# Zero fills of a gradient kernel: fifteen instead of thirteen with 8 KB rows, and whole heads in one transfer

## Chip, cores, metric

One core of one Trainium2 chip. The metric is the device time of the whole kernel in microseconds (us). It is the median of several executions.

## The reference, cut

The kernel computes one decode step of a block (attention with a sliding window, then a gated FFN) and all of its gradients. What matters here is the size of two of the outputs:

```python
Hq, Hkv, Sk, Dh = 16, 8, 32768, 256
W = min(4096, max(256, Sk // 4))                     # 4096
k = jnp.repeat(k_cache[:, :, Sk - W:, :], rep, axis=1)
v = jnp.repeat(v_cache[:, :, Sk - W:, :], rep, axis=1)
...
_out, _vjp = jax.vjp(_f, A_x, A_k_cache, A_v_cache, A_wq, A_wo, B_w_gate, B_w_up, B_w_down)
```

Only the last 4096 of 32768 positions of each cache are read, so seven eighths of both cache gradients are zero. They are outputs nevertheless: 2 x 8 x 28672 x 256 bf16 values, 234.9 MB of zeros out of 280.6 MB that the kernel writes.

## The kernel before

The zeros come from an on-chip tile of 128 partitions x 16 KB. A "block" of zeros is 128 rows of 16 KB, 2.097 MB; a head of one output has seven blocks. GpSimd's queue (`ZQ`) carries most of the fills. SyncE's queue (`LD`) carries loads, results and a few late fills.

```python
ZW = 8192
HALF0, HALF1 = 42, 55
GROUP = 4
...
def send_fills(n0, n1, halves=False):
    while n0 < n1:
        o, g, i = fills[n0]
        n = 1
        while n < GROUP and n0 + n < n1 and fills[n0 + n][:2] == (o, g):
            n += 1
        reg = zero_rows(o, g, i, i + n, ZW)
        if halves:                       # each 16 KB row as twice the lower 8 KB of the tile
            for r in range(n):
                ZQ.dma_start(out=reg[r].rearrange("p (k f) -> p k f", k=2), in_=zeros[:, 0:ZW // 2].unsqueeze(1).to_broadcast([128, 2, ZW // 2]))
        elif n == 1:
            ZQ.dma_start(out=reg[0], in_=zeros)
        else:
            ZQ.dma_start(out=reg.rearrange("n p f -> p n f"), in_=zeros.unsqueeze(1).to_broadcast([128, n, ZW]))
        n0 += n

send_fills(0, HALF0)                     # 42 blocks, 16 KB rows
send_fills(HALF0, HALF1, True)           # 13 blocks, 8 KB rows: "half fills"
# ... attention; in the FFN stage the upper half of the zero tile holds a block of weights ...
            if n == 1:
                nc.vector.memset(ar(ZW // 2, ZW // 2), 0.0)      # L443: upper half is zero again
                send_fills(HALF1, len(fills) - 1)                # the rest, 16 KB rows
# ... at the end: the last block in four pieces (L673, GpSimd), late fills (L680, SyncE)
```

A fill is only issued while fewer than eight transfers of its queue are open; the ninth waits for the first to land. In the trace of the kernel before, eight go out from 5.1 us on and the ninth at 40.5 us, after a wait for a landing.

Of the kernel before, what the change touches and what calls it, by code (L numbers as in the profile page):

```python
# [24 lines left out]
EPS = 1e-5  # L25
SCALE = 1.0 / 16.0
ZW = 8192
HALF0, HALF1 = 42, 55
GROUP = 4
NZ = (Sk - W) * Dh // (128 * ZW)  # L30
KB = 512

# [2 lines left out]
def kernel(  # L35
# [93 lines left out]
# [6 lines that stand above are left out]
# [575 lines left out]
```

## Time and profile before

| | before |
|---|---|
| time | 796.63 us median of 4 (795.74 to 797.07) |
| span of the traced execution | 796.7 us (this execution took 798.43 us) |
| moved by DMA | 334.75 MB, 420 GB/s on average |
| busy: PE, DVE, ACT | 59%, 52%, 25% |
| GpSimd's queue (q0), SyncE's queue (q1) | 216.01 MB, 116.68 MB |

The page's part 2 cuts the span into 40 slices and gives, for each, how full the DMA engines were and what they moved; its lines, and those of the hole in the middle, are shown with the prediction. How to read them: with the DMA engines at their 430 GB/s nearly everywhere, the time is bytes over rate, and only places where the rate is lower can be won back. One such place lies near 380 us.

### The profile page before, as it was taken

To read this page: it belongs to the slowest core of one execution; us is meant where nothing else is said; L and a number is where in the kernel's file an instruction comes from. 1 tells how busy PE (TensorE), PEld (TensorE's weight loads), DVE (VectorE), ACT (ScalarE), POOL (GpSimd) and SP (SyncE) were. 2 spreads that over 40 slices of the span, in tenths; PEclk is the share of its full clock that TensorE was granted. 3 is DMA by queue.
4 is the path that set the end of the run, shared out by engine and by line. 5 is a ranking of instruction groups with operands and counts; after the bars stand their busy time and mean duration, and the time that the engine had idled before them with its cause. 6 is when DMAs were issued, how large, how long until landed. Compare 5 with 4: busy or idle time off the path is not lost.

```text
span 796.7 us, 7253 instructions
## 1 busy us (share of the span) xinstructions
PE 470.7 (59%) x2926; PEld 218.9 (27%) x2926; DVE 410.4 (52%) x621; ACT 196.0 (25%) x309; POOL 35.4 (4%) x52
## 2 busy tenths in 40 slices
PE   0359998999999999353227658583450553361000
PEld 0233433344343433141116524241110211130000
DVE  2106673846648475152883488377661584472200
ACT  0043223142240301000101217372330343162200
POOL 5000000000000000100300000000000000010000
PEclk9988999999999999755557969796565556685555
DMA  9999999999999999999899999999999999999997
GB/s 349 429 431 429 429 431 430 429 430 431 429 429 430 424 425 423 416 421 422 349 421 406 429 428 428 430 431 428 426 425 432 424 429 427 427 422 410 428 443 327
DMA packets 28680, 334.75 MB, mean 420 GB/s; under 512 B 2143, under 2 KB 5223, under 8 KB 7143
## 3 DMA queue, kind: packets, MB, share of 16 engines
q0 software_dynamic: 15824, 216.01, 64.0%
q1 hardware_dynamic: 11382, 116.68, 34.9%
q10 hardware_dynamic: 1440, 1.61, 0.6%
q8 instruction: 23, 0.38, 0.2%
q14 instruction: 11, 0.08, 0.0%
HBM read 53.69 MB, written 280.59 MB: 420 GB/s over the span
## 4 chain that ended last, share of the span: by engine, by line
another core or an unknown queue 36%; DMA 29%; DVE 14%; PE 9%; issue 2%; POOL 1%; ACT 1%; DVEq 0%; ACTq 0%; SPq 0%; POOLq 0%
DMA out_dram<-arena 29%; DVE arena L469 2%; DVE arena L658 2%; DVE arena L554 2%; PE rows_ps L266 2%; PE dqb_ps L512 2%; DVE arena L659 2%; PE d_ps L651 2%; PE tr_ps L263 1%; DVE arena L524 1%; DVE arena L438 1%; POOL out_dram L138 1%; PE dqb_ps L515 1%; DVE arena L623 1%
## 5 line engine op out<-in xcount | busy, mean ns | idle before, releaser
L322 DVE TENSOR_TENSOR arena<-arena,p_f 128x2048 bf16<-128x2048 bf16 x64 | 145.3, 2286 | 64.9 <-PE M_ps L327 64.8
L327 PE MATMUL M_ps<-arena 128*128 128x512 bf16 x512 | 129.6, 382 | 0.2 <-ACT arena L333 0.2
L651 PE MATMUL d_ps<-arena 32*128 32x512 bf16 x256 | 44.8, 507 | 104.8 <-DVE arena L659 90.3
L263 PE MATMUL tr_ps<-ident_bf,arena 128*128 128x128 bf16 x1024 | 90.6, 238 | 20.0 <-DMA arena<-in_A_k_cache_dram 12.3
L266 PE MATMUL rows_ps<-arena,vpad 128*16 128x512 bf16 x256 | 87.3, 436 | 22.1 <-DVE arena L623 16.1
L263 PEld LDWEIGHTS <-arena 128*128 128x128 bf16 x1024 | 67.0, 106 | 72.8 <-issue 59.2
L280 ACT COPY arena<-tr_ps 128x1024 bf16<-128x1024 bf16 x64 | 61.8, 1016 | 69.9 <-PE tr_ps L263 69.9
L330 PE MATMUL ok_ps<-arena 128*16 128x512 bf16 x256 | 63.8, 381 | 0.9 <-DVE arena L307 0.9
L655 ACT CAST arena<-d_ps 128x512 bf16<-128x512 f32 x64 | 37.7, 588 | 103.4 <-PE d_ps L651 103.4
L327 PEld LDWEIGHTS <-arena 128*128 128x128 bf16 x512 | 43.4, 99 | 59.2 <-issue 23.5
L621 ACT COPY arena<-tr_ps 128x1024 bf16<-128x1024 bf16 x32 | 32.5, 1016 | 108.1 <-PE tr_ps L263 48.3
L659 DVE CAST arena<-d_ps 128x512 bf16<-128x512 f32 x64 | 43.5, 679 | 20.8 <-DMA out_dram<-arena 20.8
L658 DVE CAST arena<-d_ps 128x512 bf16<-128x512 f32 x64 | 43.8, 684 | 16.1 <-PE d_ps L651 15.6
L651 PEld LDWEIGHTS <-arena 32*128 32x128 bf16 x256 | 10.6, 95 | 129.9 <-issue 80.0
L656 ACT CAST arena<-d_ps 128x512 bf16<-128x512 f32 x64 | 38.2, 596 | 22.0 <-DMA out_dram<-arena 22.0
L266 PEld LDWEIGHTS <-vpad 128*16 128x16 bf16 x256 | 18.7, 91 | 57.7 <-issue 49.5
L330 PEld LDWEIGHTS <-arena 128*16 128x16 bf16 x256 | 19.1, 89 | 41.5 <-issue 20.4
L142 POOL DMA_DIRECT2D out_dram<-arena x25 | 19.3, 775 | 230.3 <-DMA out_dram<-arena 230.2
L549 DVE TENSOR_SCALAR arena<-arena,xT 128x1792 bf16<-128x1792 bf16 (+1 forms) x9 | 7.7, 881 | 35.5 <-DMA out_dram<-arena 35.5
L295 ACT ACTIVATE e_f<-cols_ps,nbias 128x32 f32<-128x32 f32 x16 | 4.5, 285 | 86.8 <-DVE nbias L291 86.8
L524 DVE CUSTOM_DVE_ANT_0 arena<-arena 128x4096 bf16<-128x4096 bf16 x3 | 13.1, 4423 | 23.2 <-ACT arena L517 23.2
L268 DVE COPY arena<-rows_ps 16x512 f32<-16x512 f32 x16 | 10.8, 676 | 27.5 <-PE rows_ps L266 27.5
(199 smaller groups left out, 388.6 us busy)
## 6 DMA issues: line engine op xcount, KB each, us to landing
out_dram<-arena POOLq DMA_DIRECT2D x13, 8192.0 KB, 167.9
out_dram<-arena POOLq DMA_DIRECT2D x12, 6144.0 KB, 171.5
out_dram<-arena SPq DMA_DIRECT2D x18, 2048.0 KB, 26.7
out_dram<-arena POOLq DMA_DIRECT2D x14, 2048.0 KB, 59.6
arena<-in_A_v_cache_dram SPq DMA_DIRECT2D x10, 2048.0 KB, 52.7
arena<-in_A_k_cache_dram SPq DMA_DIRECT2D x8, 2048.0 KB, 31.9
out_dram<-arena SPq DMA_DIRECT2D x4, 4096.0 KB, 29.9
arena<-in_A_wq_dram SPq DMA_DIRECT2D x2, 3072.0 KB, 21.3
```

Of the source, the lines that this page charges most:

```text
L263: nc.tensor.transpose(tr_ps[:, dh, i, :], X_sb[:, 4 * q + i, dh * 128:(dh + 1) * 128], ident_bf[:])
L266: nc.tensor.matmul(rows_ps[:], lhsT=pad[:, dh, 16 * q:16 * q + 16], rhs=XT[:, dh].rearrange("p t k -> p (t k)"), start=(q == 0 and dh == 0 ...
L280: sT_ps = dots(kv_at(K_off[g]), KT_slot, vpad[g % 2], rows1, ps_c, "cols", lambda q, XT, ps: nc.scalar.copy(out=XT, in_=ps))
L322: nc.vector.tensor_tensor(out=pK, in0=K_sb[:, 4 * c:4 * c + 4, :].unsqueeze(2).to_broadcast([128, 4, 2, Dh]), in1=p_f[:, c::8, :].unsqueez ...
L327: nc.tensor.matmul(M_ps[:, vh, :], lhsT=V_sb[:, t, vh * 128:(vh + 1) * 128], rhs=pK[:, i, :, :].rearrange("p h d -> p (h d)"), start=(t == ...
L330: nc.tensor.matmul(ok_ps[:].rearrange("p k d -> p (k d)"), lhsT=ppad[g % 2][:, 8 * (t % 4) + t // 4, :], rhs=both(g, t), start=(g == 0 and ...
L621: nc.scalar.copy(out=XT, in_=ps)
L651: nc.tensor.matmul(d_ps[:, qi].rearrange("p w d -> p (w d)"), lhsT=rTm[32 * q:32 * (q + 1), l, :], rhs=R_sb[32 * q:32 * (q + 1), :], start ...
L655: nc.scalar.copy(out=stV[:, t:t + 2, :], in_=d_ps[:, :, 0, :])
L656: nc.scalar.copy(out=stK[:, t:t + 2, :], in_=d_ps[:, :, 1, :])
L658: nc.vector.tensor_copy(out=stV[:, t:t + 2, :], in_=d_ps[:, :, 0, :])
L659: nc.vector.tensor_copy(out=stK[:, t:t + 2, :], in_=d_ps[:, :, 1, :])
```

## The change

The intent: keep GpSimd's queue fed with half fills until the upper half of the zero tile is free again, and send a head's seven blocks as one transfer of 14.7 MB instead of 8.4 + 6.3 MB.

```diff
-HALF0, HALF1 = 42, 55
-GROUP = 4
+HALF0, HALF1 = 42, 57
+GROUP = 7
```

## The prediction

> **What bounds the kernel now.** I read the page's part 2 first, because it says for every fortieth of the span whether anything is full.
>
> ```profile
> DMA  9999999999999999999899999999999999999997
> GB/s 349 429 431 429 429 431 430 429 430 431 429 429 430 424 425 423 416 421 422 349 421 406 429 428 428 430 431 428 426 425 432 424 429 427 427 422 410 428 443 327
> HBM read 53.69 MB, written 280.59 MB: 420 GB/s over the span
> ```
>
> The DMA engines are full in every slice but three, while part 1 has PE at 59% and DVE at 52%. So the span is a number of bytes over a rate: 334.75 MB at the 429 GB/s of a good slice is 780.3 us, and the other 16 us are where the rate was lost. Three slices (19.9 us each) stand out. The first, at 349, is the start: 19.9 x (1 - 349/429) = 3.7 us. The last, at 327, is the drain: 4.7 us. The twentieth, at 349, is a hole in the middle of the kernel: again 3.7 us. The remaining 4 us are spread over the stages with slightly lower rates.
>
> Next the hole, in the busy times by stretches (columns: stretch, its length, PE, PEld, DVE, ACT, POOL busy, granted clock, DMA share, GB/s).
>
> ```profile
> 370.00:375.00 5.00, 2.60 (x29) 2.28 (x30) 0.00 (x0) 0.00 (x0) 0.00 (x0) 0.50 1.02 428
> 375.00:380.00 5.00, 1.06 (x13) 0.91 (x12) 3.53 (x6) 0.00 (x0) 0.00 (x0) 0.50 1.00 424
> 380.00:385.00 5.00, 0.82 (x3) 0.33 (x4) 4.55 (x12) 0.00 (x0) 1.15 (x2) 0.50 0.35 144
> 385.00:390.00 5.00, 3.35 (x22) 2.20 (x21) 3.65 (x11) 1.01 (x1) 4.71 (x7) 0.50 0.99 378
> ```
>
> From about 380.5 to 385 the DMA engines have next to nothing. The timeline of GpSimd and DVE says why (start, length, engine, line, operation, count, idle before and its releaser).
>
> ```profile
> 340.11 0.67 POOL L138 DMA_DIRECT2D out_dram<-arena  x1 [5.53 <-DMA out_dram<-arena]
> 381.79 1.76 DVE L443 MEMSET arena<- 128x2048 uint32 x1 [0.41 <-DVE hh_f L424]
> 383.85 0.55 POOL L140 DMA_DIRECT2D out_dram<-arena  x1 [43.07 <-DVE arena L443]
> 384.39 5.32 POOL L142 DMA_DIRECT2D out_dram<-arena  x7
> ```
>
> The upper half of the zero tile is lent to weights. While it is, GpSimd may only send "half" fills, which read the lower half twice in 8 KB rows (L138, thirteen of them). The last was issued at 340.1; the next fill needs the memset at L443, done at 383.5, and goes out at 383.85. The DMA view for 376 to 380 has 99.7% of the engines' time on queue 0, GpSimd's: no other queue has work here, so when the thirteenth half fill is through, the engines stop. The rest of the FFN stage is not a reason to be idle; there is simply nothing queued.
>
> Last, the end. The DMA view for 735 to 745:
>
> ```profile
> q1 hardware_dynamic: 598, 4.28, 102.9%
> q0 software_dynamic: 23, 0.00, 0.1%
> ```
>
> GpSimd's queue is dry from about 735.5 on; SyncE's queue (q1) then carries its stores and from 745 the last 14.7 MB of late zero fills (L680), with the engines full until 791. So the kernel ends when the sum of all bytes is through, provided that q1 always has work after q0 is dry.
>
> **What the Trainium skill says.** "DMA: Bandwidth & Descriptors", section "Where 436 GB/s comes from", puts the ceiling of one core's 16 engines at 435.2 GB/s; the full slices at 429 to 431 agree, and leave no rate to gain. The same page, "Issuing engines are not separate DMA queues": all queues run on the same 16 engines, so moving a fill between queues[...] changes no bytes per second; agrees. The same page, "Queues, rings and completion order": an engine takes turns between the queues that have work, a packet each. From 710 to 735, where both queues are busy, the engines' time divides 50.5% to 49.4%; agrees. "Debugging Trainium Hangs", section "4. Descriptor Overflow", warns of too many descriptors for GpSimd's 16 KiB per partition. At the 16 B per descriptor of the first page that is 1024 per engine as an estimate. The change has at most 6 x 56 + 2 x 16 = 368 row descriptors per engine in the eight open transfers, against 4 x 32 + 4 x 24 = 224 before. No run here shows the limit; I expect no trouble.
>
> **The change part by part.** The order of instructions on the other engines is the same but for semaphore numbers; only GpSimd's list differs: before, 12 full fills of 8 and 6 MB, 13 half fills, then 14 fills (2, 8 and 6 MB), 4 pieces; after, 6 full fills of 14 MB, 15 half fills, then 12 MB, five of 14 MB, 8 MB, the same 4 pieces. The bytes are the same.
>
> *Half fills, 13 to 15.* Nothing before 380 changes: the first 42 zero blocks (88 MB) precede the half fills in the same order, the weights' load waits for the same 88 MB, and L443 still ends at about 383.5. But two more half fills of 2.097 MB are behind the thirteenth. At the 424 GB/s of 375 to 380 they last 2 x 2.097 / 0.424 = 9.9 us, from 380.5 to about 390. The 12 MB fill is issued at 383.9, six microseconds before they end. The hole closes. What it was worth: in 380:385, 5 x (1 - 144/425) = 3.3 us; in 385:390, 5 x (1 - 378/425) = 0.55 us, of which I count 0.2 because the following stretches partly make up for it (390:400 has 420, 400:410 has 442). Sum 3.5 us, or 1.5 MB moved earlier. The 3.7 us from the page's slice agrees.
>
> *Price of 8 KB rows.* Between 310 and 380, with half fills and the small rows of the weights, the engines moved 420 GB/s; from 160 to 300, with 16 KB rows, 428. Even if all of that were due to 8 KB rows, 4.2 MB at 420 instead of 428 costs 0.2 us.
>
> *Larger transfers.* Eleven fewer transfers on GpSimd's queue (43 to 32). Each saves about 0.7 us of issue time on an engine whose only work is issuing; off the path. The engines were already full across every boundary between transfers (428 GB/s from 160 to 300, with several boundaries in it), so there is no bubble to remove. I count 0.1 us. The slots get coarser: the third half fill now waits for the first 14 MB to land, around 70 us, instead of 166 us. That is earlier and harmless.
>
> *Behind 390.* Queue 0 is ahead by 1.5 MB. q1's share is unaffected while both are busy, so loads, stores and compute keep their times to about 728, and the 1.5 MB shows up as queue 0 going dry earlier: at its share of about 57% in 728:735 (1.65 MB in 7 us) that is 735 to about 728.5. q1 then has the engines alone. Will it run out before the last stores at 743.5? Those two (4.19 MB) took 15.0 us to land, in which the engines moved 15 x 0.43 = 6.45 MB; so 2.26 MB were still ahead of them. With 1.5 MB gone, 0.75 MB or 1.7 us of work remain, a bit more as the stores' earlier landing also frees the compute's buffers earlier. The gain should survive, by a thin margin.
>
> Sum: 796.4 - 3.5 + 0.2 - 0.1 = 793.0 us, 0.43% faster.
>
> **The rivals.**
> *A: the gain is lost at the end.* If the tail's compute comes a few microseconds late or queue 0 goes dry earlier than I think, the engines idle between 735 and 745 for what was saved at 380. For it: the margin above of 1.7 us, and the chain of waits, which has a 12 us wait of DVE for a store at 717 to 729. Against it: that wait shortens when queue 0 goes dry. The result would be 794.5 to 796.4.
> *B: the large transfers run at another rate.* 7 rows at a distance of 2 MB rather than 4 or 3. About 174 MB (6 x 14.7 + 12.6 + 5 x 14.7, in decimal MB) go in such transfers, some 407 us at 428 GB/s, so one per cent is 4 us, as large as the whole gain. Against it: the 3 and 4 row fills, the one-piece stores and the late fills all run at 427 to 430. Result 789 to 797, and I give it one chance in ten.
> *C: descriptor generation.* 896 descriptors in one instruction: if the first is seen by the engines later, or GpSimd blocks on its ring, queue 0 pauses. At the start q1 has work, so it costs nothing; at 384 the two half fills cover it. A run dry in the middle would cost several microseconds: 797 to 802. I give it 5%.
> *D: more than the hole.* Start (3.7 us) and drain (4.7 us) are not touched, so even a perfect rate elsewhere would give about 788.
>
> **Range and chances.** The forecast is 793.0. Below it, run scatter (the three runs span 1.3 us) and a small part of D reach 790.5. Above it, A in full and scatter reach 796.5. Faster by over 2% means under 780.5 us, the time of all bytes at 429 GB/s without start and drain: 1%. Slower by over 2% needs 812 us, which only a bad form of B or C gives: 2%.
>
> **What would show it.** Right: no stretch under 400 GB/s between 375 and 395; the first full fill after L443 still issued at 383 to 385; total bytes the same; mean rate from 420 to about 422 GB/s; queue 0 dry near 728; last late fill issued 1 to 3 us earlier. Wrong: a new dip near 730 to 745 (A); 160 to 300 differing from 428 GB/s by 1% or more (B); long GpSimd DMA instructions or a dip just after a 14 MB issue (C); L443 itself moved, which would mean that the half fills and the weights' loads meet in a way I left out.

## More of the kernel before

One more view of this kernel was not in the prediction, and should have been. It is the DMA view for the stretch 400 to 420, cut into 40 pieces of half a microsecond; the line has the GB/s of each piece.

```profile
GB/s 524 524 524 492 66 492 524 524 524 295 229 524 524 524 360 164 524 524 524 459 66 524 524 524 459 229 360 524 524 524 295 229 524 524 524 393 229 426 524 524
```

The average, 433 GB/s, is as elsewhere, but most pieces are either full or nearly empty. Sixteen rows of 16 KB are 0.262 MB, which in half a microsecond is 524 GB/s: a piece holds a row of each of the 16 engines, or hardly any. A row took about 0.61 us (16 x 16,384 bytes at 430 GB/s), so about every fifth piece is skipped. I read it as 16 engines that finish their rows at the same moments, in step.

## The result

| | before | changed |
|---|---|---|
| time, median of 4 | 796.63 us | 793.39 us (793.07 to 793.96) |
| ratio | | 0.9962 (95%: 0.9944 to 0.9979) |
| span traced | 796.7 us | 791.1 us |

Ratios here and below are the mean time of one kernel's runs over that of the other's in the same rounds, so not quite the ratio of the medians quoted. The difference of the two spans, 5.6 us, is larger than that of the medians, 3.2 us: the traced execution of the kernel before was at the slow end of all runs of that kernel (794.92 to 798.89 us), that of the changed kernel ordinary (793.07 us). Read gains from the medians and only places from the traces.

Part 2 of the page of the changed kernel, and its total:

```profile
DMA  9999999999999999999999999999999999999998
GB/s 345 429 432 430 429 430 431 432 431 432 428 427 430 427 427 426 418 420 422 433 431 425 425 425 432 427 429 430 427 426 429 428 427 429 423 428 407 413 439 350
...
HBM read 53.69 MB, written 280.59 MB: 423 GB/s over the span
```

The twentieth slice, the hole, has gone from 349 to 433. Slices one and forty, start and drain, were not aimed at. The average is 423 instead of 420 GB/s for the same bytes.

The busy times by stretches of the changed kernel (columns as in the prediction):

```profile
375.00:380.00 5.00, 0.59 (x8) 0.46 (x6) 4.10 (x8) 0.00 (x0) 0.00 (x0) 0.50 1.01 428
380.00:385.00 5.00, 1.39 (x4) 0.46 (x5) 4.52 (x12) 0.00 (x0) 1.72 (x2) 0.50 1.01 424
385.00:390.00 5.00, 3.03 (x20) 2.06 (x19) 3.40 (x10) 1.50 (x3) 3.99 (x5) 0.50 1.03 434
```

Where there were 144 and 378 GB/s, there are 424 and 434. GpSimd's timeline shows how:

```profile
346.17 0.68 POOL L138 DMA_DIRECT2D out_dram<-arena  x1 [5.42 <-DMA out_dram<-arena]
351.88 0.68 POOL L138 DMA_DIRECT2D out_dram<-arena  x1 [5.03 <-DMA out_dram<-arena]
383.29 5.71 POOL L142 DMA_DIRECT2D out_dram<-arena  x6 [30.72 <-DVE arena L443]
```

The two added half fills go out at 346 and 352, as slots come free. The memset releases the full fills at 383.3, half a microsecond from where it did before (383.85). So the wait on L443 ends where it did before; the engines just have something to do until then.

By the DMA view, the stretch 380 to 400 moved 8.63 MB instead of 6.81 MB.

A second thing went with the hole. The pieces of half a microsecond from 400 to 420, in the changed kernel:

```profile
GB/s 426 492 426 426 360 459 459 459 393 426 426 426 459 459 393 393 459 426 459 459 426 360 459 426 492 393 426 426 426 459 459 393 393 459 426 459 459 426 360 459
```

The pattern of full and empty pieces is gone: these engines finish their rows at different moments. And the stretch that follows, in which SyncE's queue begins to load weights beside the fills, is first for the kernel before, then for the changed one:

```profile
420.00:430.00 10.00, 6.71 (x25) 4.52 (x26) 4.75 (x23) 1.01 (x1) 0.74 (x1) 0.54 0.99 377
```

```profile
420.00:430.00 10.00, 7.28 (x26) 5.01 (x27) 4.18 (x21) 1.01 (x1) 0.00 (x0) 0.52 1.00 423
```

Part of that dip is made up for at once. Over 420 to 500 the DMA view has 33.84 MB before and 34.12 MB after, a difference of 0.28 MB or 0.7 us at 430 GB/s.

Near the end, the changed kernel has a new dip. Its DMA view for 735 to 745, and its busy times by stretches for 740 to 745:

```profile
q1 hardware_dynamic: 387, 3.91, 92.5%
```

```profile
740.00:745.00 5.00, 0.76 (x8) 0.11 (x4) 2.58 (x4) 2.15 (x4) 0.00 (x0) 0.50 0.84 353
```

GpSimd's queue is dry by then (0.21 MB in 728 to 735, against 1.65 MB before), and SyncE's gets its last stores only at 742.9 us. At 430 GB/s the five microseconds lack 0.9 us.

### The profile page after: what moved, and what is told of

Its sections match the earlier page's. It is cut to its first block, busy times and chain, and to the rows that moved or that the text cites. A ratio compares the mean times of both kernels' runs of the same rounds, so it can differ in the third digit from the quotient of the medians.

```text
span 791.1 us, 7239 instructions
## 1 busy us (share of the span) xinstructions
PE 475.9 (60%) x2926; PEld 220.8 (28%) x2926; DVE 410.6 (52%) x621; ACT 196.1 (25%) x309; POOL 29.8 (4%) x41
## 4 chain that ended last, share of the span: by engine, by line
another core or an unknown queue 40%; DMA 25%; DVE 14%; PE 10%; issue 2%; POOL 2%; ACT 1%; DVEq 0%; ACTq 0%; SPq 0%; POOLq 0%
DMA out_dram<-arena 25%; DVE arena L469 2%; PE rows_ps L266 2%; DVE arena L658 2%; DVE arena L554 2%; PE dqb_ps L512 2%; DVE arena L659 2%; PE d_ps L651 2%; PE tr_ps L263 1%; DVE arena L524 1%; DVE arena L438 1%; POOL out_dram L138 1%; PE dqb_ps L515 1%; DVE arena L623 1%
## 5 line engine op out<-in xcount | busy, mean ns | idle before, releaser
L263 PE MATMUL tr_ps<-ident_bf,arena 128*128 128x128 bf16 x1024 | 92.2, 241 | 20.2 <-DMA arena<-in_A_k_cache_dram 12.7
L266 PE MATMUL rows_ps<-arena,vpad 128*16 128x512 bf16 x256 | 89.5, 445 | 21.4 <-DVE arena L623 15.9
L623 DVE COPY arena<-tr_ps 128x1024 bf16<-128x1024 bf16 x32 | 21.8, 683 | 3.0 <-PE tr_ps L263 2.5
```

What stands on the lines that cost most here:

```text
L263: nc.tensor.transpose(tr_ps[:, dh, i, :], X_sb[:, 4 * q + i, dh * 128:(dh + 1) * 128], ident_bf[:])
L266: nc.tensor.matmul(rows_ps[:], lhsT=pad[:, dh, 16 * q:16 * q + 16], rhs=XT[:, dh].rearrange("p t k -> p (t k)"), start=(q == 0 and dh == 0 ...
```

## The experiments

Eleven runs were made, of ten other kernels and of the changed one again, all correct, in three groups, each on one chip with its own runs of the kernel before (medians 796.73, 796.48 and 796.70 us). All are the kernel before with other values of the two constants, but where the diff says otherwise. The theory: the gain is the hole near 380, and two half fills close it. The rival: the large transfers bring the gain, or take part of it.

### Half fills alone

```diff
-HALF0, HALF1 = 42, 55
+HALF0, HALF1 = 42, 57
```

> Fifteen half fills, transfers cut into 4 and 3 blocks as before. Theory (the two extra half fills are the whole gain): about 793.3 us, 0.4% under the kernel before, and the stretch 380 to 385 at over 400 GB/s. Rival (the 14 MB transfers bring the gain): about 796.6 us, as before.

Measured: 793.84 us, ratio 0.9969 (0.9956 to 0.9982). Its stretches 380 to 385 and 385 to 390:

```profile
380.00:385.00 5.00, 2.02 (x5) 0.57 (x6) 4.74 (x13) 0.00 (x0) 2.78 (x4) 0.50 1.01 429
385.00:390.00 5.00, 2.87 (x20) 2.07 (x19) 2.91 (x8) 1.77 (x3) 1.70 (x3) 0.50 1.01 428
```

The changed kernel, run in the second group, has 0.9967: the half fills alone give the whole gain. They do so without a new dip near the end (429 GB/s in 735 to 745, against 391 in the changed kernel).

### Large transfers alone

```diff
-GROUP = 4
+GROUP = 7
```

> Thirteen half fills as before, whole heads in one transfer. Theory: about 796.5 us, and the hole at 380 to 385 is still there at about 144 GB/s. Rival (large transfers bring the gain): about 793.3 us; rival (large transfers cost something that the half fills hid): over 797.5 us.

Measured: 799.04 us, ratio 1.0031 (1.0014 to 1.0048), with runs from 795.93 to 800.64. The hole is where it was:

```profile
380.00:385.00 5.00, 0.89 (x3) 0.34 (x4) 4.55 (x12) 0.00 (x0) 1.22 (x2) 0.50 0.38 161
385.00:390.00 5.00, 3.35 (x22) 2.18 (x20) 3.58 (x11) 1.01 (x1) 5.00 (x6) 0.50 0.95 364
```

So large transfers do not bring the gain. That they make this kernel 2.3 us slower agrees with the second rival's number, and was not my theory's. Up to 780 us its traced execution has moved as much as that of the kernel before (329.48 and 329.51 MB). But that one was itself 1.8 us above its kernel's median, so the traces do not show where the 2.3 us went. A later experiment takes this up.

### One half fill more instead of two

```diff
-HALF0, HALF1 = 42, 55
+HALF0, HALF1 = 42, 56
```

> Fourteen half fills, transfers as before. One half fill lasts 2.1 MB / 0.424 = 4.9 us, from 380.5 to 385.4, and the next fill is issued at 383.9, so one is just enough. Theory (the hole alone counts): 793.3 to 793.8 us, all or nearly all of the gain. Rival (each half fill is worth the same, half of the gain each): 794.9 us.

Measured: 793.77 us, ratio 0.9969 (0.9958 to 0.9981). One half fill gives all of the gain. Its stretch 380 to 385:

```profile
380.00:385.00 5.00, 2.03 (x5) 0.57 (x6) 4.73 (x11) 0.00 (x0) 2.78 (x4) 0.50 1.01 429
```

The rival that half fills are worth something each is out: it is the hole that counts, and 4.9 us of traffic cover it.

The margin is thin, though. The changed kernel was traced twice, and the kernel with the late fill moved (below) is the same code up to here: in these three traces the first full fill goes out at 383.3, 384.7 and 385.8 us, while one half fill lasts to about 385.4 by the estimate above.

### Two half fills fewer

```diff
-HALF0, HALF1 = 42, 55
+HALF0, HALF1 = 42, 53
```

> Eleven half fills, transfers as before: two half fills fewer than the kernel before. Theory (what the engines idle near 380 is lost for good, since all later time is full): the hole grows by 4.2 MB / 0.424 = 9.9 us, less 1 or 2 us because the weights of the FFN stage meet less traffic and the memset comes earlier: 804 to 806.5 us. Rival (there is slack behind it that takes it up): 796.6 to 799 us.

Measured: 806.36 us, ratio 1.0122 (1.0103 to 1.0141), 9.9 us more than before, the upper end of what was expected.

```profile
370.00:375.00 5.00, 2.53 (x30) 2.27 (x31) 0.00 (x0) 0.00 (x0) 0.00 (x0) 0.50 0.37 152
375.00:380.00 5.00, 1.00 (x12) 0.84 (x12) 3.59 (x6) 0.00 (x0) 0.00 (x0) 0.50 0.01 3
380.00:385.00 5.00, 0.88 (x3) 0.34 (x4) 4.55 (x12) 0.00 (x0) 1.21 (x2) 0.50 0.00 0
```

The hole now lasts from about 372 to 385. The memset did not come earlier (it begins at 381.73, against 381.79): the one or two microseconds that I had taken off were not there. Two half fills at 424 GB/s are 9.9 us, and 9.9 us were lost; nothing later takes them up.

### Six half fills more than the changed kernel

```diff
-HALF0, HALF1 = 42, 55
-GROUP = 4
+HALF0, HALF1 = 42, 63
+GROUP = 7
```

> Twenty-one half fills with groups of 7: the changed kernel with six more half fills than it has. Theory: once the hole is closed more half fills gain nothing; 8 KB rows are at most 1% slower, 12.6 MB at that is 0.3 us at most, so 793.2 to 794 us, equal to the changed kernel in the same rounds. Rival (half fills are better by themselves, because they leave other queues more room): 791 us or less.

Measured: 794.48 us, ratio 0.9978 (0.9965 to 0.9990), 1.0 us above the changed kernel of the same rounds. It was expected to cost 0.3 us at most, from rows that are 1% slower (half fills alone moved 424 GB/s in 375 to 380, against 428 in 160 to 300). If more than enough half fills are a small loss, the overlapping intervals do not establish it.

### The changed kernel again, and a late fill moved to GpSimd

> The changed kernel once more, for comparison in the same rounds: 793.4 us, 0.996 of the kernel before; its stretch 735 to 745 below 410 GB/s again if the early dry queue is a regular part of it, 425 or more if it was one execution's scatter.

Measured: 793.48 us, ratio 0.9967 (0.9954 to 0.9979). The dip is regular: 354 GB/s in 740 to 745, as in the first trace (353). With 424 GB/s in 735 to 740 the ten microseconds average 389, below the 410 that was to tell.

```diff
 (against the changed kernel)
-    late_jobs = [(out_2, G - 1, 5, 7, 2 * ZW), (out_3, G - 1, 0, 6, 2 * ZW), (out_3, G - 1, 6, 7, ZW)]
+    late_jobs = [(out_3, G - 1, 0, 6, 2 * ZW), (out_3, G - 1, 6, 7, ZW)]
...
-            fills += [(o, g, i) for i in range(5 if g == G - 1 else NZ)]
+            fills += [(o, g, i) for i in range(NZ)]
```

> The changed kernel, with the late fill of 4 MB of out_2 moved from SyncE's queue to the end of GpSimd's last transfer (8 MB becomes 12 MB). Theory (part of the gain is lost where GpSimd's queue is dry before the last stores, 391 GB/s at 735 to 745, worth 0.9 us): GpSimd's queue stays busy to about 746, that stretch returns to about 428 GB/s, 792.4 us, 0.9 us under the changed kernel. Rival (the dip there is of no weight, or the stores then land later and the end moves with them): 793.3 us or more.

Measured: 793.30 us, ratio 0.9965 (0.9953 to 0.9978). In 740 to 745 the dip is gone:

```profile
740.00:745.00 5.00, 1.49 (x12) 0.33 (x12) 3.28 (x6) 2.67 (x6) 0.00 (x0) 0.50 1.05 427
```

Over 735 to 745 there are 415 GB/s, against 391 and 389 in the two traces of the changed kernel, so about two thirds of the dip are closed. But the time is the same within 0.2 us. The traces show where the lead went. Up to 780 us this execution had moved 331.79 MB, against 331.54 and 331.48, which is 0.6 to 0.7 us of work. By 788 us all three had moved 334.7 MB, and the spans are 791.9, 791.1 and 791.5 us: the lead was lost in the drain. A possible reason: the average over 16 engines falls while some have run out, and the last engine, which sets the end, was not among them. The profile does not tell the engines apart, so this is argued and not shown. Nor is the other half of the rival ruled out: the last pair of stores did go out later, at 746.1 us against 742.9 and 743.1. And with the scatter of five runs each, a gain of half a microsecond could be missed.

### Single blocks, and groups of two

```diff
-HALF0, HALF1 = 42, 55
-GROUP = 4
+HALF0, HALF1 = 42, 57
+GROUP = 1
```

> Fifteen half fills, and every full fill a transfer of 2 MB of its own, some 100 instead of 28 on GpSimd's queue. Theory (transfer size has no price while eight are open): about 793.3 to 793.8 us. Rival (each transfer has a price of its own, larger ones save it): slower than the fifteen half fills with groups of 4 or 7, by at least 0.1 us a transfer, so over 800 us.

Measured: 796.84 us, ratio 1.0010 (0.9997 to 1.0023). There is no hole (429 GB/s in 380 to 385; the memset begins at 375.3 us here, against 380.2 with groups of 4), yet the gain is gone. So smaller transfers do have a price, 3.0 us for 62 more of them. It is neither nothing, as I had expected, nor 0.1 us each.

```diff
-HALF0, HALF1 = 42, 55
-GROUP = 4
+HALF0, HALF1 = 42, 57
+GROUP = 2
```

> Fifteen half fills, groups of 2: 68 transfers on GpSimd's queue, against 44 with groups of 4 (793.84 us) and 106 with single blocks (796.84 us). If each transfer has a price of (796.84 - 793.84) / 62 = 0.048 us: 793.84 + 24 x 0.048 = 795.0 us. If only the smallest transfers are slow (too little open work in eight of them): 793.8 us.

Measured: 796.00 us, ratio 0.9991 (0.9979 to 1.0004). Both expectations missed: against groups of 4, 24 more transfers cost 2.2 us by the medians (of different chips) and 1.8 us by the ratios. Whether the price is one amount per transfer stays open: by the ratios it is 0.07 us each here and 0.05 us each for the 62 above, and the intervals leave room for both to be equal.

The traces show one thing that changes steadily with the size. In the stretch 420 to 710 both queues are at work, and GpSimd's line in the DMA view (packets, MB, share of the engines' time) reads, for groups of 7 (the changed kernel), 4 (half fills alone), 2 and 1:

```profile
q0 software_dynamic: 5056, 81.31, 66.0%
```

```profile
q0 software_dynamic: 5078, 80.38, 65.3%
```

```profile
q0 software_dynamic: 5183, 79.25, 64.6%
```

```profile
q0 software_dynamic: 5372, 78.24, 63.9%
```

The smaller its transfers, the less GpSimd's queue gets done while it competes. It is not one trace's scatter: all seven traces with groups of 7 have 80.9 to 81.8 MB there, all four with groups of 4 80.4 to 80.7. The other queue gets most of it, so its stores come earlier: the last pair of results but one (L661) goes out at 720.9 us with groups of 7 (717.3 in the second trace of that kernel), 714.8 with 4, 710.3 with 2 and 704.9 with 1. The total moved up to 780 us falls as well, against groups of 4 by 0.44 MB with groups of 2 and 0.93 MB with single blocks, or 1.0 and 2.2 us at 430 GB/s. The rest lies in a longer drain, for which no cause was found.

### Large transfers with the large hole

```diff
-HALF0, HALF1 = 42, 55
-GROUP = 4
+HALF0, HALF1 = 42, 53
+GROUP = 7
```

> Eleven half fills and whole heads in one transfer: the kernel with the large hole (806.4 us, 1.0122 of the kernel before) but with groups of 7. If large transfers cost 2 to 3 us whenever the engines stood still before them, as the kernel with large transfers alone seemed to show: 808.5 to 809.5 us, a ratio of about 1.015. If that was scatter of the kernels with a hole: a ratio of 1.010 to 1.013.

Measured: 807.99 us, ratio 1.0143 (1.0127 to 1.0158), between the two expectations, and 1.0122 (1.0103 to 1.0141) with groups of 4, on another chip. The intervals overlap. Together with the kernel with large transfers alone, it points to a small price of large transfers where there is a hole; where there is none, no price is seen (0.9962 and 0.9967 for the changed kernel against 0.9969 and 0.9969 with groups of 4 and two or one half fills more). The cause stays open.

### The least that closes the hole, with the late fill moved

```diff
 (against the kernel with the late fill moved)
-HALF0, HALF1 = 42, 57
+HALF0, HALF1 = 42, 56
```

> Fourteen half fills (just enough), groups of 7, and the 4 MB late fill on GpSimd's queue. If the six extra half fills of the earlier run cost 1.0 us (0.17 us each), one fewer gains 0.2 us, and the early transfer of the late fill gains the 0.2 us that it showed: 793.0 us, not distinguishable from the changed kernel's 793.4. If the slowest DMA engine sets the end, nothing here moves it: 793.4 us.

Measured: 793.48 us, ratio 0.9963 (0.9950 to 0.9976). No version tried is better than the changed kernel by a resolved amount.

## Why the prediction was right

The forecast was 793.0 us with a range from 790.5 to 796.5; measured were 793.39 us. The mechanism was right. That the number came so close is in part luck: in the traces more was moved earlier than forecast, and the medians do not show all of it as gain (below).

*The hole and its worth: right.* The half fills close it, the wait at L443 stays, and the gain of 3.2 us matches the forecast of 3.4. The kernels with one half fill more and with two fewer show the mechanism by dose: the first added one gives everything, the second nothing, and the two removed cost, together, their full 9.9 us. The signs named beforehand came too: the first full fill went out at 383.3 us, and the last late fill 1.3 us earlier than before (747.8 against 749.1).

*The size of 1.5 MB moved earlier: too small.* From 380 to 400 the traces differ by 1.82 MB, and by another 0.28 MB from 420 to 500, together 2.1 MB or 4.9 us. The step that missed it took the hole for a plain pause. What followed the pause, engines in step and a dip when the loads begin, was in the table of stretches (377 GB/s in 420 to 430) and I passed over it. The two traces differ by 4.9 us there and the medians by 3.2 us. How much of this is the slow traced execution of the kernel before (1.8 us above its median) and how much was lost at the end, the record does not show.

*The price of 8 KB rows, 0.2 us for two: not contradicted.* Six more cost 1.0 us, or 0.3 us for two, but the overlapping intervals do not show that it is more than nothing.

*Larger transfers, 0.1 us: right for this change, with an argument that does not hold.* I said that full engines across the boundaries leave nothing to remove. With groups of 1 the engines look as full in short stretches (429 GB/s in 380 to 385) and are nearly so in long ones (426 in 160 to 300, against 428), and with groups of 2 and 1 about 2 and 3 us are lost. From 4 to 7 no gain is resolved.

*Behind 390, "q1's share is unaffected while both are busy": wrong.* With larger transfers GpSimd's queue took more, and SyncE's last pair of results but one left at 720.9 us (717.3 in the second trace), against 714.8 with the half fills alone and 715.9 before. GpSimd's queue went dry near 728 as forecast, but partly for this reason. With it, rival A happened: the thin margin of 1.7 us was not there, and the engines idled in part at 740 to 745. With the half fills alone it did not happen.

*Rival A's cost, 1.5 to 3.4 us: wrong.* The dip came, and the time was still 793.39 and 793.48 us, not 794.5 or more. Closing two thirds of it moved the time by 0.2 us, and the kernel with the half fills alone, which has no dip, is no faster (793.84 us).

*Rivals B and C: did not happen.* From 160 to 300 the rate was 429 GB/s against 428, and no dip follows the issue of the 14 MB transfers. The eight open transfers ran without trouble. By the prediction's own count of rows they come to 376 per engine, not 368: from 391 us on, seven full fills and one half fill are open.

*Two readings of the lines were off, without weight for the sum.* By the digits the engines are busy in every slice but two, not three: the first slice has a 9, so its 349 GB/s is a low rate and not an idle stretch. And the third half fill went from 204.0 us to 71.0; 166 us was the place of the first.

## What to carry to other kernels

Where the DMA engines are full nearly everywhere, as here, a pause in the middle is not made up for later: 9.9 us of added pause at 370 us cost 9.9 us at the end. Look for a pause in the row of GB/s, and ask which queue could have had a transfer waiting. Put enough work before the blocking wait: here the first transfer that covered the pause brought everything and further ones nothing, though the end of the wait scattered by 2.5 us between executions, which speaks for one in reserve. The size of transfers also shifted how two busy queues share the engines, and so when buffers came free elsewhere.

## What the Trainium skill lacked or had wrong

- "DMA: Bandwidth & Descriptors", section "Queues, rings and completion order", has engines take turns between queues packet by packet. It does not say that the share of a queue also depends on how its work is cut into transfers: with rows unchanged, GpSimd's queue moved 81.31, 80.38, 79.25 and 78.24 MB in the same 290 us with groups of 7, 4, 2 and 1 blocks. Why is not shown.
- The same page, section "Rules for kernel authors", asks for 1 MiB or more per transfer for the most bandwidth. It says nothing of how much is left above that size with several transfers open. Here kernels with transfers of 2.1 and 4.2 MB, eight of them open, were still some 3 and 2 us slower in 795 us than those with 6.3 and 8.4 MB (ratios 1.0010 and 0.9991 against 0.9969). From there to 14.7 MB no further gain was resolved.
- No page has it that engines fall in step after a pause. In the kernel before, which has the hole, 16 engines finished rows together for tens of microseconds, by my reading of the pieces (66 to 524 GB/s), and the start of loads beside the fills then gave 377 GB/s in 420 to 430. All four kernels with a hole show that pattern in 400 to 420 and had 377 to 392 GB/s in 420 to 430; all nine traces without one lack it and had 410 to 424. That being in step causes the dip is not shown.
